# Chunked retention and two feed-forward layers: quarter-array products, and another cut and order of the feed-forward groups

## The chip, the cores and the metric

One core of one Trainium2 chip. The metric is the device time of one execution in microseconds (us), the median of several runs. The kernel before: 912.83 us, the median of 3 runs (910.53 to 913.34).

## The reference

Retention (attention without softmax, with a decay) over 4 batches, 8 heads, 576 tokens, 64 features a head; its output, 2304 tokens by 512 features, goes through two feed-forward layers of 2048 hidden features. Everything is float32.

```
scores = (q @ k.T) / sqrt(64)
ret    = scores * where(i >= j, gamma[h] ** (i - j), 0)
x      = (ret @ v)                        # heads side by side: 2304 x 512
h = x @ w_in;  x = (h * sigmoid(h)) @ w_out
h = x @ w2_in; out = (max(h, 0) + alpha * min(h, 0)) @ w2_out
```

## The kernel before, in words

**Retention.** The 2304 tokens are 18 blocks of 128; a block of 1 MB holds q and k with features on the partitions, and k and v with tokens on the partitions. A block n takes four products, in float32: the scores (`att_scores`, L227: 8 matmuls, 64 rows of the array by 128 columns, 128 tokens streamed), what comes from earlier tokens through a state of 64 x 64 a head ("cross", first loop of `att_out`, L255: 8 matmuls of 64 x 64, 128 tokens streamed), what comes from within the block ("inside", L263: 8 matmuls of 128 x 64, 128 streamed), and the state's update (`att_state`, L268: 8 matmuls of 128 x 64, 64 streamed, accumulated in one PSUM bank over a whole batch). The profile shows a float32 matmul as two passes, each with its weight load. VectorE (DVE) multiplies the scores by a mask, in two halves (L238); GpSimd (POOL) multiplies q by decays (L221) and v by inverse decays (L225); ScalarE (ACT) copies the output (L266) and the state (L277) out of PSUM. The loads go over SyncE's (SP) DMA queue into three buffers.

**Feed-forward.** The tokens are five tiles (256, 512, 512, 512, 512). The 16 hidden feature tiles of a layer are worked in groups of four: for a group and a token tile, four h units (12 matmuls each) and then four y units (`y_unit`, layer 0) or one out unit for each 128 tokens (`out_unit`, layer 1), of 12 matmuls each, which add to what the earlier groups left. Every operand is split into a high and a low float32r part, so that a product takes three matmuls. A token tile is split by `split_x` (L282; ACT copies, DVE subtracts at L288), four times for each group and tile; an h unit ends with a sigmoid on ACT, a product on DVE (L302), a copy on ACT and a difference on DVE (L311).

**Weights.** They come as 64-bit numbers and are converted on the chip: for each weight tile of 128 x 512 two ACT operations, and on DVE a shift (L175), a sign (L180), a mask (L187), a rest (L194) and a low part (L198), with an ACT copy between and a POOL product (L189). These are the jobs of `w_jobs`; `spread` hangs them behind units of the program.

**What sets the order.** The program is a list, `units`, each with the jobs that follow it in `after`; every engine works its own instructions in the order of that list. Blocks stand between units by hand (L407 to L450). The first group needs eight weight tiles; the weights of group g+1 are converted while group g runs over its tiles (L467 to L475).

Of the kernel before, what the change touches and what calls it, by code (L numbers as in the profile page):

```python
# [9 lines left out]
F32 = mybir.dt.float32  # L10
# [8 lines left out]
P = 128  # L19
# [16 lines left out]
def starts_batch(blk):  # L36
    return (blk * P) % S == 0


def boundary(blk):  # L40
    return (blk * P) // S != (blk * P + P - 1) // S


def ends_batch(blk):
    return (blk * P + P) % S == 0
# [14 lines left out]
def retention_ffn_kernel(ctx: ExitStack, tc: tile.TileContext, qkv, w1, w2, alpha, qtab, small, out):  # L60
# [13 lines left out]
    ps = ctx.enter_context(tc.tile_pool(name="ps", bufs=7, space=bass.MemoryType.PSUM))  # L74
    ps_state = ctx.enter_context(tc.tile_pool(name="ps_state", bufs=1, space=bass.MemoryType.PSUM))
# [26 lines left out]
    rings = {k: Ring() for k in ("w0", "w1", "x", "g", "act", "down", "pr")}  # L102
# [4 lines left out]
    rings["act"].grow(big, "act", NMAX, 2)  # L107

# [5 lines left out]
    right = ctx.enter_context(tc.tile_pool(name="right", bufs=1, side="right"))  # L114
    rings["w0"].grow(right, "w0b_", 512, 4, F32R)
    rings["w1"].grow(right, "w1b_", 512, 4, F32R)
    early_pool = ctx.enter_context(ExitStack())
    early = early_pool.enter_context(tc.tile_pool(name="early", bufs=1, side="right"))

    qtab_sb = att.tile([P, NPAIR, S], F32, name="qtab_sb")  # L120
    small_sb = att.tile([P, 2 * P + PERIOD * H], F32, name="small_sb")
    masks = small_sb[:, 0:2 * P].rearrange("p (b t) -> p b t", b=2)
    vtab = small_sb[:, 2 * P:].rearrange("p (n h) -> p n h", h=H)
    state = [att.tile([P, NPAIR, D], F32, name=f"state{i}") for i in range(2)]
    rings["pr"].grow(att, "pr", 4 * P, 4)
    PACK = 4 * DM
    over = NC * NT - 2 * PACK
    packs = [bufb[:, over:over + PACK], bufb[:, over + PACK:], early.tile([P, PACK], F32, name="pack")]

    def pack(n):  # L130
        return packs[n % len(packs)].rearrange("p (s a) -> p s a", s=4)

    def close_att():
        early_pool.close()
        pool = ctx.enter_context(tc.tile_pool(name="weights", bufs=1, side="right"))
        rings["w1"].grow(pool, "w1c_", 512, 4, F32R)
# [8 lines left out]
    def psum(name):  # L145
        return ps.tile([P, 512], F32, tag="ps", name=name)
# [5 lines left out]
    def w_ahead(upto, queue=None):  # L152
        for i in range(len(raws), min(upto, len(worder))):
            layer, kind, f = worder[i]
            raws[i] = stage.tile([P, 512], I64, tag="raw", name="raw", bufs=RAWS)
            (queue or (nc.sync if i < 2 * GF else nc.scalar)).dma_start(out=raws[i], in_=(w1, w2)[layer][kind, f])
# [52 lines left out]
    probs = {}  # L209
    x_hi, x_lo = {}, {}  # L210
    kv = ps_state.tile([P, 512], F32, name="kv")[:, 0:NPAIR * D].rearrange("p (c d) -> p c d", c=NPAIR)
# [3 lines left out]

    def att_prep_q(n, engine):
        q = pack(n)[:, 0].rearrange("p (c t) -> p c t", c=NPAIR)
        at = n * P % S
        for lo, hi in ((0, S - at), (S - at, P)) if at + P > S else ((0, P),):
            a = (at + lo) % S  # L220
            engine.tensor_tensor(out=q[:, :, lo:hi], in0=q[:, :, lo:hi], in1=qtab_sb[:, :, a:a + hi - lo], op=ALU.mult)  # L221

    def att_prep_v(n, engine):
        v = pack(n)[:, 3].rearrange("p (h d) -> p h d", h=H)
        engine.tensor_tensor(out=v, in0=v, in1=vtab[:, n % PERIOD].unsqueeze(2).to_broadcast([P, H, D]), op=ALU.mult)  # L225

    def att_scores(n):  # L227
        q, k = (pack(n)[:, i].rearrange("p (c t) -> p c t", c=NPAIR) for i in range(2))
        sc = [psum("sc").rearrange("p (c t) -> p c t", c=NPAIR) for _ in range(2)]
        for p in range(NPAIR):  # L230
            for j in range(2):
                r = slice(j * D, (j + 1) * D)
                nc.tensor.matmul(sc[j][:, p], k[r, p], q[r, p], start=True, stop=True, skip_group_check=True)  # L233
        mask = masks[:, int(boundary(n))].unsqueeze(1).to_broadcast([P, NPAIR, P])
        probs[n] = []
        for j in range(2):
            pr = rings["pr"].next().rearrange("p (c t) -> p c t", c=NPAIR)
            nc.vector.tensor_tensor(out=pr, in0=sc[j], in1=mask, op=ALU.mult)  # L238
            probs[n].append(pr)

    def att_out(n):
        at = n * P
# [3 lines left out]
        xo = [psum("xo")[:, 0:2 * P].rearrange("p (c t) -> p c t", c=2) for _ in range(2)]  # L246
        begun = set()

        def mm(j, p, cols, lhsT, rhs):
            half = p % 2  # L250
            nc.tensor.matmul(xo[j][half * D:(half + 1) * D, p // 2, 0:cols], lhsT, rhs,  # L251
# [3 lines left out]
        if not starts_batch(n):  # L255
            cols = D if boundary(n) else P
            for p0 in range(0, NPAIR, 2):
                for j in range(2):
                    for p in (p0, p0 + 1):
                        r = slice(j * D, (j + 1) * D)  # L260
# [7 lines left out]
    def att_state(n):  # L268
        if ends_batch(n):
            return  # L270
# [292 lines left out]
```

## Time and profile before

| what | value |
|---|---|
| median of 3 runs | 912.83 us |
| the profiled execution's own time | 912.46 us |
| its span, first to last instruction | 910.7 us |
| mean granted TensorE clock | 0.981 |
| TensorE (PE) busy | 870.2 us (96%) |
| DVE busy | 586.6 us (64%) |
| ACT busy | 434.9 us (48%) |
| POOL busy | 133.7 us (15%) |
| HBM, mean over the span | 64 GB/s |

Busy shares are means over a span of two parts: the stretch in which retention and the first group share the core, up to about 177 us, and the feed-forward after it. The 1.8 us between the profiled time and the span lie outside the instructions.

### The profile page before, as it was taken

How to read it: one execution, taken by the hardware profiler on the slowest of the kernel's cores; microseconds unless marked ns; L12 is line 12 of the kernel's file. 1: busy time of each engine (PE TensorE's matmuls, PEld its weight loads, DVE VectorE, ACT ScalarE, POOL GpSimd, SP SyncE). 2: the span in 40 equal slices, each digit the busy share in tenths (PEclk: the TensorE clock that was granted, in tenths of full speed). 3: DMA queues.
4: the chain of work that ended last, by engine and by line, in shares of the span. 5: the costliest groups of instructions: out<-in, count | busy, mean ns of one | idle time of the engine just before them, and what ended most of it. 6: DMA issues, size and time to landing. Idle time of an engine off the chain costs nothing.

```text
span 910.7 us, 12282 instructions
## 1 busy us (share of the span) xinstructions
PE 870.2 (96%) x4844; PEld 725.4 (80%) x4844; DVE 586.6 (64%) x954; ACT 434.9 (48%) x845; POOL 133.7 (15%) x104
## 2 busy tenths in 40 slices
PE   5749979999999999999999999999999999999998
PEld 4648857788888888888888888888888888888887
DVE  3984354666876677766775666655786677665442
ACT  2534444555543355434544476656555465545340
POOL 2750242210110011110110011010111011100000
PEclk9778989999999999999999999999999999999999
DMA  8630534111211011101101011001201011000102
GB/s 322 223 139 31 177 141 135 60 47 40 70 47 47 1 69 53 41 24 47 62 32 46 1 70 62 32 24 46 70 24 47 24 69 48 24 1 37 55 25 93
DMA packets 18539, 59.31 MB, mean 65 GB/s; under 512 B 2096, under 2 KB 3504, under 8 KB 18480
## 3 DMA queue, kind: packets, MB, share of 16 engines
q10 hardware_dynamic: 8064, 29.36, 9.3%
q1 hardware_dynamic: 10416, 29.15, 9.0%
q8 instruction: 38, 0.62, 0.3%
q14 instruction: 21, 0.17, 0.1%
HBM read 53.78 MB, written 4.72 MB: 64 GB/s over the span
## 4 chain that ended last, share of the span: by engine, by line
PE 90%; DVE 6%; DMA 2%; ACT 1%; issue 1%; SPq 0%; POOL 0%; ACTq 0%; DVEq 0%; POOLq 0%
PE ph L298 14%; PE ph L296 14%; PE ph L297 14%; PE py L321 7%; PE py L322 7%; PE py L323 7%; PE po L342 7%; PE po L341 7%; PE po L340 7%; PE xo L251 2%; PE sc L233 2%; DVE w L198 1%; DMA qtab_sb<-in_qtab 1%; DMA raw<-in_w 1%; DVE a L180 1%; DVE a L194 1%
## 5 line engine op out<-in xcount | busy, mean ns | idle before, releaser
L189 POOL TENSOR_TENSOR low<-low,top 128x512 f32<-128x512 f32 x64 | 89.8, 1404 | 594.2 <-DVE top L187 543.6
L296 PE MATMUL ph<-x,w 128*128 128x512 f32 (+1 forms) x440 | 163.6, 372 | 0.6 <-ACT x L287 0.6
L298 PE MATMUL ph<-x,w 128*128 128x512 f32 (+1 forms) x440 | 163.0, 370 | 1.3 <-DVE x L288 1.3
L297 PE MATMUL ph<-x,w 128*128 128x512 f32 (+1 forms) x440 | 162.7, 370 | 0.0
L298 PEld LDWEIGHTS ph<-x,w 128*128 128x128 f32 x440 | 83.6, 190 | 16.3 <-DVE x L288 2.5
L296 PEld LDWEIGHTS ph<-x,w 128*128 128x128 f32 x440 | 83.8, 190 | 15.3 <-ACT x L287 1.0
L311 DVE TENSOR_TENSOR g<-act,g 128x512 fp32r<-128x512 f32 (+1 forms) x88 | 59.2, 673 | 57.0 <-ACT g L310 57.0
L297 PEld LDWEIGHTS ph<-x,w 128*128 128x128 f32 x440 | 83.8, 190 | 13.9
L307 DVE SCALAR_TENSOR_TENSOR act<-down,nalpha_sb,act 128x512 f32<-128x512 f32 (+1 forms) x80 | 58.9, 737 | 52.6 <-ACT act L306 51.7
L310 ACT CAST g<-act 128x512 fp32r<-128x512 f32 (+1 forms) x88 | 51.2, 582 | 85.2 <-DVE act L302 46.8
L311 DVE TENSOR_TENSOR gb<-act,gb 128x512 fp32r<-128x512 f32 (+1 forms) x72 | 47.2, 655 | 46.0 <-ACT gb L310 46.0
L301 ACT ACTIVATE act<-ph 128x512 f32<-128x512 f32 (+1 forms) x80 | 44.2, 552 | 68.3 <-PE ph L298 68.0
L298 PE MATMUL ph<-x,w0b 128*128 128x512 f32 (+1 forms) x200 | 74.4, 372 | 0.2 <-DVE x L288 0.2
L296 PE MATMUL ph<-x,w0b 128*128 128x512 f32 (+1 forms) x200 | 74.5, 372 | 0.0
L310 ACT CAST gb<-act 128x512 fp32r<-128x512 f32 (+1 forms) x72 | 41.3, 573 | 69.5 <-DVE act L307 39.9
L297 PE MATMUL ph<-x,w0b 128*128 128x512 f32 (+1 forms) x200 | 74.4, 372 | 0.0
L302 DVE TENSOR_TENSOR act<-ph,act 128x512 f32<-128x512 f32 (+1 forms) x80 | 50.8, 634 | 36.3 <-ACT act L301 35.6
L305 ACT ACTIVATE down<-ph 128x512 f32<-128x512 f32 (+1 forms) x80 | 44.1, 551 | 58.8 <-PE ph L298 58.8
L288 DVE TENSOR_TENSOR x<-bufa,x 128x512 fp32r<-128x512 f32 (+1 forms) x80 | 57.3, 721 | 14.6 <-ACT x L287 13.9
L288 DVE TENSOR_TENSOR x<-bufb,x 128x512 fp32r<-128x512 f32 (+1 forms) x80 | 53.1, 664 | 13.7 <-ACT x L287 13.0
L188 ACT CAST w<-a 128x512 fp32r<-128x512 f32 x38 | 23.6, 620 | 70.5 <-DVE a L180 70.5
L321 PE MATMUL py<-g,w 128*128 128x512 f32 (+1 forms) x128 | 48.3, 377 | 7.0 <-ACT g L310 7.0
(129 smaller groups left out, 1860.8 us busy)
## 6 DMA issues: line engine op xcount, KB each, us to landing
raw<-in_w ACTq DMA_DIRECT2D x56, 512.0 KB, 3.2
bufb<-in_qkv SPq DMA_DIRECT2D x24, 512.0 KB, 5.5
pack<-in_qkv SPq DMA_DIRECT2D x12, 512.0 KB, 5.6
out<-bufa SPq DMA_DIRECT2D x17, 256.0 KB, 2.0
raw<-in_w SPq DMA_DIRECT2D x8, 512.0 KB, 4.4
qtab_sb<-in_qtab SPq DMA_DIRECT2D x1, 896.0 KB, 8.4
qtab_sb<-in_qtab SPq DMA_DIRECT2D x1, 256.0 KB, 5.1
out<-bufa SPq DMA_DIRECT2D x2, 128.0 KB, 1.7
```

What stands on the lines that cost most here:

```text
L189: nc.gpsimd.tensor_tensor(out=low, in0=low, in1=top, op=ALU.mult)
L288: nc.vector.tensor_tensor(out=lo, in0=src, in1=f32(hi), op=ALU.subtract)
L296: nc.tensor.matmul(o, wh[:, cs], hi[:, c, 0:n], start=c == 0, stop=False)
L297: nc.tensor.matmul(o, wl[:, cs], hi[:, c, 0:n], start=False, stop=False)
L298: nc.tensor.matmul(o, wh[:, cs], lo[:, c, 0:n], start=False, stop=c == NC - 1)
L310: nc.scalar.copy(gh[:, 0:n], g)
L311: nc.vector.tensor_tensor(out=gl[:, 0:n], in0=g, in1=f32(gh[:, 0:n]), op=ALU.subtract)
L321: nc.tensor.matmul(o, wh[:, ms], gh, start=f == fs[0], stop=False)
L322: nc.tensor.matmul(o, wl[:, ms], gh, start=False, stop=False)
L323: nc.tensor.matmul(o, wh[:, ms], gl, start=False, stop=f == fs[-1])
L340: nc.tensor.matmul(o, gh[:, bs], wh[:, ms], start=f == fs[0], stop=False)
L341: nc.tensor.matmul(o, gh[:, bs], wl[:, ms], start=False, stop=False)
```

## The change

The state is carried from 64 tokens to 64 (`C`, `NCH` = 9 chunks a batch). All four products become 16 matmuls of 64 x 64 that stream 64 columns (8 where a chunk begins or ends a batch), each in one quarter of the array. The decay goes into a table with the mask (`dtab`), applied to the scores in one DVE operation; POOL scales k (`att_prep_k`) instead of v; q is scaled after the scores have read it; its table is built on the chip by one DVE product of 128 x 2048 (`att_tables`). The state's updates are added on DVE, one operation of 128 x 256 for each chunk, and ACT no longer copies the state. A step n (`att_step`) is one unit: cross and half of inside for block n, scores of n+1, the other half of inside, state of n+1, load of block n+4. The blocks have four buffers instead of three. `split_block` splits the 128 tokens of each block behind its step. In PSUM, four single banks serve the units and states, and two pairs the scores and outputs; after retention all eight are single.

Layer 0 has five groups, of 2, 4, 4, 4 and 2 feature tiles, layer 1 four of 4. The order of the tiles turns round at each group of a layer, and the tile at the turn keeps its split x. A unit of a 2-tile group has 6 matmuls in y (h units stay at 12). A step stands behind single units of tiles 0 to 3. A 4-tile group behind a 2-tile group has all eight weight tiles converted ahead of it, else six ahead and two behind.

```diff
-GF = 4
-NG = NF // GF
+C = 64
+NCH = S // C
+GROUPS = [(0, range(0, 2)), (0, range(2, 6)), (0, range(6, 10)), (0, range(10, 14)), (0, range(14, 16)),
+          (1, range(0, 4)), (1, range(4, 8)), (1, range(8, 12)), (1, range(12, 16))]
+PACKS = 4
...
+    def att_scores(n, engine):
+        sc = banks()
         for p in range(NPAIR):
             for j in range(2):
+                for c in range(2):
+                    nc.tensor.matmul(sc[rows(c), j, p * C:(p + 1) * C], k[rows(j), p, rows(c)], q[rows(j), p, rows(c)],
+                                     start=True, stop=True, skip_group_check=True)
+        nc.vector.tensor_tensor(out=probs[n], in0=sc[:, :, 0:NPAIR * C], in1=dtab, op=ALU.mult)
+        att_prep_q(n, engine)
+    def att_state(n):
...
+                for c in cs:
+                    nc.tensor.matmul(up[c][rows(j), p * D:(p + 1) * D], k[rows(c), 2 * p + j], v[rows(c), 2 * p + j],
+                                     start=True, stop=True, skip_group_check=True)
...
+                nc.vector.tensor_tensor(out=new, in0=up[c][:, 0:NPAIR * D], in1=states[g], op=ALU.add)
...
+    def att_step(n):
+        out = att_out(n)
+        next(out)
+        if n + 1 < NBLK:
+            att_prep_k(n + 1, nc.gpsimd)
+            att_scores(n + 1, nc.gpsimd)
+        for _ in out:
+            pass
+        if n + 1 < NBLK:
+            att_state(n + 1)
+        if n + PACKS < NBLK:
+            att_load(n + PACKS)
...
+    for s in range(1, len(TILES)):
+        more = range(n, min(n + 4, NBLK))
+        n += 4
+        first.append(add(hs[s][0]))
+        for i, unit in enumerate(hs[s][1:] + ys[s][0:3]):
+            if i < len(more):
+                at[more[i]] = step(more[i])
+            add(unit)
...
+    spread(w_jobs(0, 2), at[0], first[0])
+    spread(w_jobs(2, 4), first[0], y0)
+    lo, mid = wcut[1]
+    spread(w_jobs(lo, lo + 4), first[1], closed)
+    spread(w_jobs(lo + 4, mid), closed, first[T] + 1)
+    for gi in range(2, len(GROUPS)):
+        lo, mid = wcut[gi]
+        hi = wcut[gi + 1][0]
+        start, end = first[T * (gi - 1)], first[T * gi - 1]
+        spread(w_jobs(lo, mid), first[T * (gi - 1) + 1] + 2, end)
```

On PE, a block's products stand as follows before (block 6 with its neighbours; `sc` scores, `xo` with `state` cross, `xo` with `pr` inside, `kv` the state):

```order
L233 MATMUL sc<-bufb 128x128 x8
L251 MATMUL xo<-bufb,state_123 64x128 x8
L251 MATMUL xo<-pr_125,bufb 64x128 x4
L251 MATMUL xo<-pr_126,bufb 64x128 x4
L275 MATMUL kv<-bufb 64x64 x8
```

And a step now (step 3; the last row stands for the state of a block that ends a batch; in other steps it has 16 matmuls in two banks by turns):

```order
L283 MATMUL two_109<-pack_127,state_120 64x64 x8
L283 MATMUL two_109<-pack_127,state_121 64x64 x8
L283 MATMUL two_109<-pr_119,pack_127 64x64 x8
L245 MATMUL two_108<-bufb 64x64 x16
L283 MATMUL two_109<-pr_119,pack_127 64x64 x8
L259 MATMUL bank_104<-bufb 64x64 x8
```

The forms 128x128 and 64x128 (columns by tokens streamed) are gone; matmuls are 64 now where they were 32.

On DVE, in layer 0, the rows around the second h unit of a tile while the next group's weights are converted, before (L302 and L311 end an h unit, L328 adds a y unit, L288 splits x, the others are weight jobs):

```order
L302 TENSOR_TENSOR act_103<-ph,act_103 128x512
L311 TENSOR_TENSOR g_97<-act_103,g_96 128x512
L288 TENSOR_TENSOR x_93<-bufa,x_92 128x512
L180 SCALAR_TENSOR_TENSOR a<-top,a 128x512
L187 TENSOR_SCALAR top<-a 128x512
L328 TENSOR_TENSOR bufb<-py,bufb 128x512
L288 TENSOR_TENSOR x_93<-bufa,x_92 128x512
L194 TENSOR_TENSOR a<-a,w_2_76 128x512
L328 TENSOR_TENSOR bufb<-py,bufb 128x512
```

And in the last group of layer 0, of two feature tiles, now (L358 and L367 end an h unit, L383 adds a y unit, L335 splits x, L180 to L203 are weight jobs):

```order
L367 TENSOR_TENSOR g_96<-act_99,g_95 128x512
L185 SCALAR_TENSOR_TENSOR a<-top,a 128x512
L192 TENSOR_SCALAR top<-a 128x512
L199 TENSOR_TENSOR a<-a,w0b_1760 128x512
L383 TENSOR_TENSOR bufb<-bank_104,bufb 128x512
L335 TENSOR_TENSOR x_90<-bufa,x_89 128x512
L203 TENSOR_TENSOR w0b_1761<-a,low 128x512
L180 TENSOR_SCALAR a<-top 128x512
L383 TENSOR_TENSOR bufb<-bankb_1774,bufb 128x512
L335 TENSOR_TENSOR x_90<-bufa,x_89 128x512
```

Two or three weight operations stand behind every unit now, where one stood, and a y unit between two L383 rows has 6 matmuls instead of 12.

## Rows read from the trace of the kernel before

**Rows 1.** Busy time by stretch: start:end, length, busy of each engine, clock, DMA.
```profile
core 0: us, PE busy (x) PEld busy (x) DVE busy (x) ACT busy (x) POOL busy (x), PEclk, DMA share, GB/s
23.00:46.00 23.00, 16.44 (x212) 14.68 (x214) 21.34 (x30) 12.02 (x29) 16.42 (x13) 0.78 0.63 219
46.00:69.00 23.00, 11.56 (x94) 9.99 (x93) 19.46 (x28) 7.88 (x20) 11.11 (x8) 0.72 0.37 136
...
300.00:400.00 100.00, 100.00 (x486) 83.94 (x485) 71.30 (x122) 45.47 (x85) 10.96 (x8) 1.00 0.13 43
```

**Rows 2.** Waits of PE: for whom, us in total, times, longest.
```profile
PE sc L233 <- DVE bufb L221: 10.6, 2, 7.2
PE xo L251 <- ACT state L277: 9.1, 4, 3.9
```

**Rows 3.** The chain that ended last, in order of time: start us, us, what.
```profile
68.12 0.58 PE py L322
...
85.98 1.09 PE sc L233 x16
87.07 1.62 PE xo L251 x32
88.69 0.47 PE kv L275 x16
...
176.88 0.43 PE py L321
177.31 0.23 PE py L322
...
907.11 0.12 PE po L340
907.50 0.42 DVE bufa L347
```

**Rows 4.** The timeline of PE: cross products of 128 and of 64 streamed columns.
```profile
87.00 0.67 PE L251 MATMUL xo<-bufb,state 64*64 64x128 f32 x16
...
150.69 0.46 PE L251 MATMUL xo<-bufb,state 64*64 64x64 f32 x16
```

**Rows 5.** DVE by line and shape, 12 to 69 us: busy us, mean ns, idle before.
```profile
L198 DVE TENSOR_TENSOR w<-a,low 128x512 fp32r<-128x512 f32 x8 | 10.1, 1257 | 0.9 <-DVE a L194 0.5
L238 DVE TENSOR_TENSOR pr<-sc,small_sb 128x512 f32<-128x512 f32 x12 | 7.7, 680 | 5.1 <-PE sc L233 5.1
L194 DVE TENSOR_TENSOR a<-a,w 128x512 f32<-128x512 f32 x8 | 7.4, 922 | 0.0
L180 DVE SCALAR_TENSOR_TENSOR a<-top,a 128x512 int32<-128x512 int32 x8 | 7.2, 897 | 0.2
L175 DVE TENSOR_SCALAR a<-top 128x512 int32<-128x512 int32 x8 | 6.1, 762 | 1.2 <-ACT top L167 0.8
L187 DVE TENSOR_SCALAR top<-a 128x512 int32<-128x512 int32 x8 | 3.4, 423 | 0.2
L288 DVE TENSOR_TENSOR x<-bufa,x 128x256 fp32r<-128x256 f32 x4 | 2.1, 544 | 0.0
```

**Rows 6.** POOL by line, 12 to 69 us.
```profile
L189 POOL TENSOR_TENSOR low<-low,top 128x512 f32<-128x512 f32 x8 | 12.2, 1528 | 15.2 <-DVE top L187 15.2
L225 POOL TENSOR_TENSOR bufb<-bufb,small_sb 128x512 f32<-128x512 f32 x5 | 6.3, 1268 | 5.2 <-DMA bufb<-in_qkv 5.2
```

**Rows 7.** DVE by line and shape, 400 to 500 us.
```profile
L288 DVE TENSOR_TENSOR x<-bufa,x 128x512 fp32r<-128x512 f32 x16 | 12.9, 806 | 0.7 <-ACT x L287 0.4
L328 DVE TENSOR_TENSOR bufb<-py,bufb 128x512 f32<-128x512 f32 x16 | 10.9, 685 | 6.2 <-PE py L323 6.2
L311 DVE TENSOR_TENSOR g<-act,g 128x512 fp32r<-128x512 f32 x9 | 6.2, 692 | 6.2 <-ACT g L310 6.2
L180 DVE SCALAR_TENSOR_TENSOR a<-top,a 128x512 int32<-128x512 int32 x8 | 5.5, 685 | 0.1
L187 DVE TENSOR_SCALAR top<-a 128x512 int32<-128x512 int32 x8 | 3.4, 423 | 0.1
```

**Rows 8.** The timeline at the start: start us, us, instruction, idle before.
```profile
8.16 1.04 POOL L225 TENSOR_TENSOR bufb<-bufb,small_sb 128x512 f32<-128x512 f32 x1 [7.72 <-DMA bufb<-in_qkv]
```

More of the change, by code (lines that the diff above doesn't have):

```diff
@@ L268, in att_state @@
-    def att_state(n):
-        if ends_batch(n):
-            return
-        kt, v = (pack(n)[:, i].rearrange("p (h d) -> p h d", h=H) for i in (2, 3))
-        r0 = D if boundary(n) else 0
-        for p in range(NPAIR):
-            for j in range(2):
-                nc.tensor.matmul(kv[j * D:(j + 1) * D, p], kt[r0:, 2 * p + j], v[r0:, 2 * p + j],
-                                 start=p == 0 and (starts_batch(n) or boundary(n)), stop=True, skip_group_check=True)
-        nc.scalar.copy(state[(n + 1) % 2], kv)
+                        mm(j, p, c, v[rows(c), 2 * p + j], pr[rows(c), j, p])
@@ L288, in split_x, with split_block @@
         nc.vector.tensor_tensor(out=lo, in0=src, in1=f32(hi), op=ALU.subtract)
[L290 to L291 removed]
+    def split_block(b):
+        t = next(i for i, (a, m) in enumerate(SPANS) if a <= b * P < a + m)
+        at = b * P - SPANS[t][0]
+        src = acts(bufa, *SPANS[t])[:, :, at:at + P]
+        hi, lo = (t[:, :, at:at + P] for t in x_tiles((0, t)))
+        nc.scalar.copy(hi, src)
+        nc.vector.tensor_tensor(out=lo, in0=src, in1=f32(hi), op=ALU.subtract)
@@ L411, in retention_ffn_kernel @@
-    marks = []
-    for f in range(GF):
-        if f == 0:
-            first.append(len(units))
-        add(hs[0][f])
-        if f < 2:
-            A[4 + f] = block(4 + f)
-    marks.append(len(units))
-    add(*ys[0])
-    first.append(len(units))
-    add(*hs[1])
-    for n in (6, 7):
-        A[n] = block(n)
-    add(*ys[1])
-    A[8] = block(8)
-    for n in (9, 10):
-        A[n] = block(n)
-    first.append(len(units))
-    add(*hs[2])
-    for n in (11, 12):
-        A[n] = block(n)
@@ L432, in retention_ffn_kernel, with step @@
-    add(*ys[2])
-    for n in (13, 14):
-        A[n] = block(n)
-    first.append(len(units))
-    add(*hs[3])
-    for n in (15, 16, 17):
-        A[n] = block(n)
-    closed = len(units)
-    add(close_att)
-    add(*ys[3])
-    first.append(len(units))
-    add(*hs[4])
-    prev = list(ys[4])
+        wcut.append((len(worder), len(worder) + len(a[:early] + b)))
+        worder += a[:2] + b[:2] + a[2:] + b[2:] if gi == 1 else a[:early] + b + a[early:]
+    wcut.append((len(worder),) * 2)
+    def step(n):
+        return add(lambda: att_step(n))
@@ new lines, in retention_ffn_kernel @@
+    hs, ys = zip(*(unit_pair(s) for s in range(len(TILES))))
+    at = {}
+    at[0] = step(0)
+    at[1] = step(1)
+    first.append(add(hs[0][0]))
+    at[2] = step(2)
+    add(hs[0][1])
+    at[3] = step(3)
+    y0 = add(*ys[0][0:2])
+    at[4] = step(4)
+    add(*ys[0][2:4])
+    at[5] = step(5)
+    n = 6
+    for s in range(1, len(TILES)):
[6 more added lines that the diff above has]
+            add(unit)
+        if s < len(TILES) - 1:
+            add(*ys[s][3:])
+        if more and more[-1] == NBLK - 1:
+            closed = add(close_att)
```

309 lines of the change are left out of this document (150 added, 159 removed).

## The prediction, made before the changed kernel had run

> **What bounds the kernel now.** I read the busy time by stretch first [rows 1]. From 300 to 400 us PE is busy for all of it at the full clock, 1.00 (2.4 GHz), and DVE for 71%: from there on only fewer or faster matmuls would help. From 23 to 69 us PE is busy for 28.0 of 46 us at a mean clock of 0.78 and 0.72, so partly at 1.2 GHz, and DVE for 40.8: there DVE sets the pace. The waits of PE [rows 2] are short of that, 10.6 us for q's product on DVE, 9.1 for the copy of the state.
>
> The chain of waits [rows 3] gives two marks. The y units of the first tile run through only from 68.12 us, when DVE has the last of eight weight tiles ready. The last product of retention ends at 176.88. By then tiles 1 and 2 and the h units of tile 3 are done, 240 matmuls of 512 columns, and tile 0, 96 of 256. A matmul of 512 columns takes 0.23 us [rows 3], one of 256 takes 0.12 (the same rows, at the end). So 240 x 0.23 + 96 x 0.12 = 66.7 us of the feed-forward are done at 176.8, and what follows takes 910.7 - 176.8 = 733.9 us to the end of the span. The number of feed-forward matmuls stays the same; I therefore ask when the changed kernel has retention behind it, how much is done by then, and whether PE is kept busy after it.
>
> **Retention on PE.** A block takes 1.09 (scores) + 1.62 (cross and inside) + 0.47 (state) = 3.18 us [rows 3]. The state's 16 passes of 64 columns stand in pairs, one in each half of the array's columns: 0.47 / 8 = 0.058 us a pair. Cross products stand in quarters already. Halving their columns takes them from 0.67 to 0.46 us [rows 4], so that four quarters do overlap, at 64 columns too: 16 passes begin and end in 0.46 us, the fill and end of the pipeline among it. With four at a time, each of the new products (32 passes) takes 8 x 0.058 = 0.46 us, four take 1.86, and with some 0.2 for going in and out between feed-forward units (an estimate, from 3.18 us a block and the 0.1 to 0.2 that the first passes of a form take longer [rows 4]) a step takes 2.05 us. The lower end is 0.67 - 0.46 = 0.21 us for four such rounds [rows 4], 0.053 each, 1.7 a step; the upper end is 32 passes at the state's 0.47 / 16 = 0.029 us, 0.94 a product, 3.75 a step, if no more than two overlap over a long run. I take 2.05, since the nearest row, the same form in quarters, shows four overlapping; the upper end is a rival below.
>
> The Trainium skill says in "TensorE: Matmul & The Clock Gate", section "Wait — 56ns, not 53.3ns?", that matmuls never start closer than about 25 ns however few their columns, and that with decoding in software each costs about 62 ns; by the first a step's 128 passes would take an estimated 3.2 us, by the second 7.9, instead of 2.05. The trace speaks against the second, as a block's 64 passes take 3.18 us, and against the first for a short burst, 16 passes within 0.46 us; for a long run no row here shows it.
>
> **The start, to the first y unit.** The first group needs four weight tiles instead of eight. Until its first y unit DVE has, in its order: four weights at 1.26 + 0.92 + 0.90 + 0.76 + 0.42 = 4.26 us each [rows 5], 17.0; five score products at 0.68 [rows 5], 3.4; nine state updates of 128 x 256, between 0.34 (half of a score product) and 0.68, taken as 0.40, 3.6; four splits of 128 x 512 at 0.85 (0.54 for 128 x 256 [rows 5], and 0.81 for 128 x 512 [rows 7]), 3.4; the ends of two h units, 2.7; the table of 128 x 2048 (four times 0.68 at most, taken as 2.3) with k and q of block 0, 3.3. The sum is 33 us. It begins at about 4 us, when the small table is in. Waits come on top, 8 us: the block's 1.0 MB and the 0.45 of tables ahead of it land at about 8.2 us (before, v of block 0 was the end of 1.45 MB and there at 8.16 [rows 8]), the first products run at half clock, and the weights' loads, now on ACT's queue, stand beside four 1 MB loads. So y begins at **45 us**, where before it ran from 68.
>
> **From there to the end of retention.** Tile 0's four y units (24 matmuls at 0.12, half of them at 1.2 GHz after the wait: 4.3), steps 4 and 5 (4.1, and 1.9 more if one runs at 1.2 GHz) and 2 for block 5's split, which the next h unit awaits at once: tile 1 begins at 57 us. Tiles 1 to 3 take each two h units (24 x 0.227 = 5.45), four y units of 6 matmuls (5.45) and four steps (8.2), 19.1 us. DVE has beside that four times 0.68 + 2 x 0.40 + 0.85 = 9.3, two h units at 0.69 + 0.69 and a wait of 0.69 for ACT between (6.2 us over nine [rows 7]), 4.1, and a third of four weights, at 4.0 each 5.4: 18.8. Both engines are full, and I add 5 us for waits, most for k on POOL, which stands behind a weight's product of 1.53 us [rows 6]. Retention is then done at 57 + 57.4 + 5 = **about 120 us** instead of 177.
>
> **What is done by then** is less, 3 x 48 x 0.227 + 48 x 0.12 = 38.5 us against 66.7: 28.2 more are left, so 733.9 + 28.2 = 762.1 us.
>
> **What two-tile groups cost.** In these groups a token tile is worth 48 x 0.23 = 11.0 us of PE, half of a four-tile group's, but the weights of the next group have to pass DVE in that time. Group 4 (the last of layer 0) has eight of them ahead of layer 1, in 16 units, 2.67 token tiles. DVE has for each token tile: two h ends at 2.07 (4.1), four additions at 0.685 (2.7), four splits at 0.81 (3.2), three weights at 2 x 0.42 + 3 x 0.685 = 2.9 (8.7) [rows 7]: 18.8, and some 17 since neighbours overlap by about 0.08. The order puts the difference that the next y unit reads behind these jobs, with one h unit of 2.76 us between on PE, so PE can't run ahead of DVE by more than about 2 us: (17 - 11) x 2.67 - 2 = **14 us** of stall, where before such a stretch was covered by PE. Behind retention, tile 4 of group 0 has four weights (11.6) and three h ends (6.2) beside 12.4 us of PE: 17.8 - 12.4 - 2 = **3 us**.
>
> The smaller edits: splits saved at the turns cost PE nothing now and give nothing while PE is full (their cover is DVE's slack of 29% there [rows 1]); a fourth block buffer spares waits for loads, which are in the 57 us between the two marks; the end (last addition 0.42 at 907.50 [rows 3], then the store) is the same, half a block.
>
> **Sum.** 120 + 762.1 + 14 + 3 = 899 us of span, and 1.8 outside it: **901 us**. The profiled execution took 912.46, the median of the runs is 912.83, so they stand alike; about 0.3%, 2.7 us, is what a measurement of this kernel can tell from no change.
>
> **The rivals.**
> *Passes come no faster than 0.029 us.* Quarters overlap in a burst, but not over 64 matmuls in a row. For it: the longest run of quarters in the trace has 16 passes, after a pause. Against it: nothing slows in that run. Its place is the 14 steps from the first y on. Each takes 3.75 + 0.2 = 3.95 instead of 2.05, 26 us in all; the 5 us of waits vanish beneath it: 901 + 26 - 5 = 922 us, slower than before. It decides from about 2.9 us a step on.
> *The copies out of PSUM and the decays hold up retention.* The order of a step puts the state's addition and q's scaling between the scores and the next cross product; where before PE waited 9.1 us in four waits for a state [rows 2], it waits now in each of 12 steps, 1 us more than I count: 913 us, no change. For it: DVE at 18.8 of 19.1. The Trainium skill's "TensorEngine Tiling (Array Packing)", section "PSUM Bottleneck", warns of this: packing speeds up TensorE, not the way out of PSUM.
> *The weights' jobs find room.* If DVE's work in the two-tile groups is covered (its queue runs ahead or ends overlap more), 14 of the 17 us go: 887 us.
> *The steps don't pack at all* would give the price of the first rival; the change's other parts stand in the order either way.
>
> **How the numbers follow.** Forecast 901 us, with 893 to 910 of its own: 50%. Passes too slow, 922: 17%. Retention held up, 913: 15%. Weights covered, 887: 18%. Faster by over 0.3% (below 910): 0.45 from the first, 0.18 from the last, 0.63. Within 0.3%: 0.05 and 0.08, 0.13. Slower: 0.17 and 0.07, 0.24. The range leaves out some 10% on either side: below, the half of the covered case that gains further in retention, above, the worse half of slow passes: 885 to 921.
>
> **What would show it.** In the new profile: a product's 32 passes in about 0.46 us, a step in about 2; the first y unit at about 45 us; retention done at about 120; gaps of PE in the last group of layer 0, some 14 us together, laid to the difference on DVE; none after it. Passes of 0.029 us, or retention past 135 us, or a full PE in that group would make the forecast wrong.

## The result, and the profile after

| what | before | after |
|---|---|---|
| median of the runs | 912.6 us (910.53 to 913.34, 4 runs) | 924.46 us (923.61 to 925.07, 4 runs) |
| ratio to before, 95% interval | | 1.0133 [1.0114, 1.0152] |
| span of the profiled execution | 910.7 us | 923.3 us |
| mean granted TensorE clock | 0.981 | 0.972 |
| PE busy | 870.2 us (96%) | 868.2 us (94%) |
| DVE busy | 586.6 us (64%) | 594.4 us (64%) |
| ACT busy | 434.9 us (48%) | 428.8 us (46%) |
| POOL busy | 133.7 us (15%) | 128.7 us (14%) |

The changed kernel is 1.3% slower than before, where 901 us, 1.3% faster, was forecast; the time lies above the range (885 to 921). I read the new profile at the marks of the forecast first, then by stretch, then by waits.

The marks, from the timeline of PE (start us, us, instruction, idle before and what ended it): the first y unit runs through from 44.47, tile 1 begins at 54.19, the last product of retention starts at 132.11, and 135.35 is the first h unit after tile 3.

```profile
44.47 0.58 PE L377 MATMUL bank<-g,w 128*128 128x256 f32 x1 [0.39 <-DVE w L203]
...
54.19 0.50 PE L352 MATMUL bank<-x,w 128*128 128x512 f32 x1 [0.68 <-ACT x L343]
...
132.11 0.46 PE L283 MATMUL two<-pr,pack 64*64 64x64 f32 x16 [0.50 <-ACT bufa L303]
...
135.35 0.39 PE L352 MATMUL bankb<-x,w 128*128 128x512 f32 x1
```

Forecast were 45, 57 and 120 for the first, second and last of these. So the start came as worked out, and the stretch from tile 1 to the end of tile 3 took 81.2 us instead of 62.4 (57.4 and 5 of waits).

PE by stretch (start:end, length, busy time, clock, DMA):

```profile
core 0: us, PE busy (x), PEclk, DMA share, GB/s
0.00:54.00 54.00, 30.30 (x832) 0.81 0.63 234
54.00:136.00 82.00, 67.39 (x1539) 0.94 0.42 143
136.00:460.00 324.00, 322.14 (x1550) 0.99 0.12 40
460.00:512.00 52.00, 41.72 (x140) 0.84 0.22 78
512.00:923.00 411.00, 406.68 (x1874) 1.00 0.12 42
```

Two stretches lose time: the one with retention, and the last group of layer 0 at 460 to 512 us. In the latter 140 matmuls, all of 512 columns, at the 0.23 us of a covered one [rows 3] are 32.2 us of 52: 19.8 us are lost, of which 10.3 with PE idle and the rest in slower matmuls at a mean clock of 0.84. The long stretches beside it are full: 1.9 us idle in 324, 4.3 in 411.

All engines in the stretch with retention:

```profile
core 0: us, PE busy (x) PEld busy (x) DVE busy (x) ACT busy (x) POOL busy (x), PEclk, DMA share, GB/s
54.00:136.00 82.00, 67.39 (x1539) 53.38 (x1540) 48.18 (x76) 36.81 (x74) 30.70 (x27) 0.94 0.42 143
```

No engine is full here. DVE is busy for 48.2 us of 82, where I had it at 18.8 of each 19.1 us, 56.4 of 57.4 (4.1 of these were waits for ACT within the h units). The time goes into waits of PE, which that stretch lists so (for whom, us in total, times, longest):

```profile
PE two L283 <- ACT bufa L303: 8.2, 8, 2.1
PE bank L259 <- POOL pack L230: 4.9, 3, 1.9
...
PE two L283 <- DVE state L267: 0.5, 1, 0.5
```

With the two rows left out, 0.7 us each, that is 15.0 us instead of 5. Over the whole span the same view has:

```profile
PE two L283 <- ACT bufa L303: 14.1, 11, 3.1
...
PE bank L259 <- POOL pack L230: 5.4, 4, 1.9
...
PE bank L259 <- POOL bufb L230: 1.8, 1, 1.8
```

These take the place of the waits of [rows 2], which are gone. The largest, for ACT's copy at L303, is not a wait for a state or for DVE. The timeline of all engines around one step that stands behind an h unit shows it (rows of the weight loads are left out):

```profile
92.78 0.69 PE L283 MATMUL two<-pack,state 64*64 64x64 f32 x32
92.89 0.60 ACT L357 ACTIVATE act<-bank 128x512 f32<-128x512 f32 x1 [1.26 <-PE bank L354]
...
93.30 0.41 PE L283 MATMUL two<-pr,pack 64*64 64x64 f32 x16
...
93.52 0.69 DVE L358 TENSOR_TENSOR act<-bank,act 128x512 f32<-128x512 f32 x1
93.53 0.65 PE L245 MATMUL two<-bufb 64*64 64x64 f32 x32
94.24 0.62 ACT L366 CAST g<-act 128x512 fp32r<-128x512 f32 x1 [0.76 <-DVE act L358]
...
94.77 0.37 ACT L303 COPY bufa<-two 128x256 f32<-128x256 f32 x1
...
95.19 0.46 PE L283 MATMUL two<-pr,pack 64*64 64x64 f32 x16 [1.01 <-ACT bufa L303]
...
95.47 0.65 PE L259 MATMUL bank<-bufb 64*64 64x64 f32 x32
...
96.04 0.50 PE L376 MATMUL bank<-g,w 128*128 128x512 f32 x1
```

A step puts out the cross products and the first half of the inside products (16 matmuls), the scores of the next block, and then the second half of inside. That half adds to the same banks from the other half of the array's rows, and the program lets ACT copy the first sums out before it. The copy stands in ACT's queue behind the end of the h unit: the sigmoid (92.89), DVE's product with it (93.52), and the cast that waits for this product (94.24). So PE waits from 94.18 to 95.19 for a copy of 0.37 us. The state's product behind it waits in other steps for k, which POOL scales.

The arithmetic itself packs. The 32 matmuls of the scores at 93.53 take 0.65 us to the end of the last; one alone is shown as 0.22 us long (the row at 87.52 us in experiment 5), so they start within 0.43 us, 14 ns apart. The ends of matmuls are modelled in a profile; the starts alone say nearly the same, 48 passes between 92.78 and 93.53, 16 ns apart. From 92.78 to 96.04 are 3.26 us, without the wait 2.25; 2.05 was forecast.

**Where the time went between the two kernels.** At the end of retention before had 66.7 us of the feed-forward done of 176.8, and now 38.5 of 135.35. So retention with all that surrounds it costs 96.9 us instead of 110.1, 13.2 less. The rest takes 923.3 - 135.35 = 787.95, less the 28.2 that it has more to do 759.8, against 733.9: 25.9 more. The difference is the 12.6 us of the two spans. The change gains in retention, though little, and gives twice as much back behind it, 19.8 us of that in one group.

### The profile page after: what moved, and what is told of

Same layout as the page of the kernel before. It is cut to its first block, busy times and chain, and to the rows that moved or that the text cites. A ratio compares the mean times of both kernels' runs of the same rounds, so it can differ in the third digit from the quotient of the medians.

```text
span 923.3 us, 14365 instructions
## 1 busy us (share of the span) xinstructions
PE 868.2 (94%) x5932; PEld 714.8 (77%) x5932; DVE 594.4 (64%) x979; ACT 428.8 (46%) x819; POOL 128.7 (14%) x102
## 4 chain that ended last, share of the span: by engine, by line
PE 84%; DVE 10%; ACT 3%; issue 1%; POOL 1%; DMA 1%; ACTq 0%; SPq 0%; DVEq 0%; POOLq 0%
PE bankb L353 9%; PE bankb L354 9%; PE bankb L352 9%; PE bank L376 7%; PE bank L377 6%; PE bank L378 6%; PE bank L354 5%; PE bank L353 5%; PE bank L352 5%; PE bankb L396 4%; PE bankb L394 4%; PE bankb L395 4%; PE bank L396 3%; PE bank L395 3%; PE bank L394 3%
## 5 line engine op out<-in xcount | busy, mean ns | idle before, releaser
L194 POOL TENSOR_TENSOR low<-low,top 128x512 f32<-128x512 f32 x64 | 89.2, 1393 | 630.5 <-DVE top L192 593.7
L354 PE MATMUL bankb<-x,w 128*128 128x512 f32 (+1 forms) x276 | 103.2, 374 | 1.9 <-DVE x L335 1.9
L353 PE MATMUL bankb<-x,w 128*128 128x512 f32 (+1 forms) x276 | 102.9, 373 | 1.5 <-DVE w L203 1.5
L352 PE MATMUL bankb<-x,w 128*128 128x512 f32 (+1 forms) x276 | 102.9, 373 | 0.0
L363 DVE SCALAR_TENSOR_TENSOR act<-down,nalpha_sb,act 128x512 f32<-128x512 f32 (+1 forms) x80 | 61.8, 772 | 51.3 <-ACT act L362 50.3
L367 DVE TENSOR_TENSOR g<-act,g 128x512 fp32r<-128x512 f32 (+1 forms) x84 | 57.4, 683 | 54.2 <-ACT g L366 54.2
L366 ACT CAST g<-act 128x512 fp32r<-128x512 f32 (+1 forms) x84 | 48.7, 579 | 78.4 <-DVE act L358 39.8
L367 DVE TENSOR_TENSOR gb<-act,gb 128x512 fp32r<-128x512 f32 (+1 forms) x76 | 48.7, 641 | 48.8 <-ACT gb L366 48.8
L357 ACT ACTIVATE act<-bankb 128x512 f32<-128x512 f32 (+1 forms) x65 | 35.9, 552 | 69.8 <-PE bankb L354 69.7
L383 DVE TENSOR_TENSOR bufb<-bank,bufb 128x512 f32<-128x512 f32 (+1 forms) x69 | 44.2, 641 | 35.4 <-PE bank L378 35.1
L353 PE MATMUL bank<-x,w 128*128 128x512 f32 (+1 forms) x164 | 60.5, 369 | 4.5 <-DVE w L203 4.5
L354 PE MATMUL bank<-x,w 128*128 128x512 f32 (+1 forms) x164 | 61.1, 373 | 3.3 <-DVE x L335 2.6
L352 PE MATMUL bank<-x,w 128*128 128x512 f32 (+1 forms) x164 | 61.3, 374 | 1.6 <-ACT x L334 0.9
L354 PEld LDWEIGHTS bankb<-x,w 128*128 128x128 f32 x276 | 51.9, 188 | 12.3 <-DVE x L335 3.2
L353 PEld LDWEIGHTS bankb<-x,w 128*128 128x128 f32 x276 | 51.9, 188 | 10.9 <-DVE w L203 1.7
L358 DVE TENSOR_TENSOR act<-bankb,act 128x512 f32<-128x512 f32 (+1 forms) x65 | 41.3, 635 | 29.0 <-ACT act L357 28.2
L352 PEld LDWEIGHTS bankb<-x,w 128*128 128x128 f32 x276 | 51.9, 188 | 9.3
L335 DVE TENSOR_TENSOR x<-bufb,x 128x512 fp32r<-128x512 f32 (+1 forms) x68 | 46.8, 689 | 9.7 <-ACT x L334 9.1
L353 PE MATMUL bankb<-x,w0b 128*128 128x512 f32 (+1 forms) x136 | 50.0, 368 | 0.0
L352 PE MATMUL bankb<-x,w0b 128*128 128x512 f32 (+1 forms) x136 | 50.0, 368 | 0.0
```

Source lines behind the costliest of these rows:

```text
L194: nc.gpsimd.tensor_tensor(out=low, in0=low, in1=top, op=ALU.mult)
L352: nc.tensor.matmul(o, wh[:, cs], hi[:, c, 0:n], start=c == 0, stop=False)
L353: nc.tensor.matmul(o, wl[:, cs], hi[:, c, 0:n], start=False, stop=False)
L354: nc.tensor.matmul(o, wh[:, cs], lo[:, c, 0:n], start=False, stop=c == NC - 1)
L363: nc.vector.scalar_tensor_tensor(out=g, in0=dn, scalar=nalpha_sb[:, f:f + 1], in1=g, op0=ALU.mult, op1=ALU.add)
L366: nc.scalar.copy(gh[:, 0:n], g)
```

## The experiments

Ratios are against before, run beside each experiment on the same chip (911.95 to 912.6 us on all of them). "After" stands for the changed kernel, 924.46 us and 1.0133.

**1. Groups of three in place of the last two-tile group.**

```diff
-GROUPS = [(0, range(0, 2)), (0, range(2, 6)), (0, range(6, 10)), (0, range(10, 14)), (0, range(14, 16)),
+GROUPS = [(0, range(0, 2)), (0, range(2, 6)), (0, range(6, 10)), (0, range(10, 13)), (0, range(13, 16)),
```

> One edit: layer 0 in groups of 2, 4, 4, 3 and 3 feature tiles instead of 2, 4, 4, 4 and 2. Ahead of layer 1 stand seven weight tiles in three quarters of a group's time, not eight in half of it. Theory A: the gaps and the half clock in the last group of layer 0 (about 14 us of gaps and 6 of clock between 463 and 510 us) come from DVE's eight weights there: they go but for 2 or 3, 906 us. Rival B: they come from something else at the change of layers (splits of x, the order of the tiles): still some 20 us there, 924 us.

Measured: 912.78 us (910.81 to 915.39, 10 runs), 1.0001 [0.9988, 1.0013], 11.7 us below after. The same place in its profile, by stretch:

```profile
core 0: us, PE busy (x), PEclk, DMA share, GB/s
457.00:512.00 55.00, 52.36 (x238) 0.97 0.12 39
```

Of these 238 matmuls 190 have 512 columns and 48 have 256. At 0.23 and 0.12 us they are 49.5 us of work in 55, so 5.5 us are lost here instead of 19.8, at a clock of 0.97. Counted by the same matmuls, from the first of the fourth group to the third h unit of layer 1, the profile has 173.1 us instead of 184.0 in after. Seven weight tiles pass DVE in the last group, instead of eight, in a group that is half as long again. More than half of the loss in that group is so shown to come from its size (the one weight fewer follows from it), and 11.7 us are nearly the whole of the difference to before.

**2. The state's products ahead of the second half of inside.**

```diff
-        for _ in out:
-            pass
         if n + 1 < NBLK:
             att_state(n + 1)
+        for _ in out:
+            pass
```

> One edit: in a step the state's products of block n+1 stand ahead of the second half of inside, not behind it. Theory A: a step loses time because the second half of inside waits for ACT's copy of the first half (14.1 us in 11 waits of the changed kernel), and that wait is counted from the end of the first half; 0.45 us more of PE work between them takes 0.45 us from each long wait and all of the short ones of 0.2: 11 x 0.45, about 5 to 6 us less, 918 to 920 us. Rival B: in retention DVE and ACT are full whatever PE does, the time returns at the next cross product or state: 924 us, unchanged. If the state then waits for k on POOL, up to 0.3 us a step come back.

Measured: 924.67 us (921.79 to 931.11, 4 runs), 1.0145 [1.0099, 1.0191]: no gain that runs so far apart can show. Its waits of PE over the span:

```profile
PE bank L259 <- POOL pack L230: 9.8, 4, 2.6
...
PE two L283 <- ACT bufa L303: 5.9, 7, 1.7
PE bank L259 <- POOL bufb L230: 5.3, 1, 5.3
```

The wait for the copy fell from 14.1 to 5.9 us, and that for k rose from 7.2 to 15.1. The two waits lay one behind the other; what stands first takes the time of both.

**3. k a step earlier on POOL.**

```diff
-            att_prep_k(n + 1, nc.gpsimd)
             att_scores(n + 1, nc.gpsimd)
+        if n + 2 < NBLK:
+            att_prep_k(n + 2, nc.gpsimd)
```

> One edit: POOL scales k of block n+2 behind q of block n+1, a step earlier, so that it no longer queues behind a weight's product that waits for DVE. Theory A: the 7.2 us that the state's products wait for POOL in the changed kernel go, but a part is only the lead of another wait in the same step: 917 to 921 us. Rival B: POOL has no time left, q comes later instead: 924 us or above.

Measured: 918.54 us (918.21 to 921.1, 4 runs), 1.0074 [1.0054, 1.0094], 5.9 us below after. No wait for POOL at L230 is left in its profile, and the other stands where it stood:

```profile
PE two L283 <- ACT bufa L303: 14.1, 11, 3.6
```

The gain is near the 7.2 us that the view gave for this wait. Not all of it is PE's idle time: between the starts of tiles 1 and 4 that falls from 14.4 to 13.1 us only, and the clock there is 1.00 instead of 0.94 (the table further down).

**4. The h unit's end queued behind the next step's first copy.** In retention the sigmoid and what follows it are put off until the step has issued its first copy:

```diff
         out = att_out(n)
         next(out)
+        while pending:
+            pending.pop(0)()
...
+        if defers[0] and (layer, f) in ((0, 0), (0, 1)):
+            pending.append(lambda: h_end(key, layer, f, n, o))
+        else:
+            h_end(key, layer, f, n, o)
```

> One edit: in retention an h unit's end (sigmoid, product, copy, difference) is issued behind the next step's first copy out of PSUM instead of ahead of it, so that this copy doesn't queue on ACT behind a copy that waits for DVE's product. Theory A: the long waits of 1.23 us that stand in the steps behind h units fall to the 0.24 of the steps behind y units; six of them in tiles 1 to 3 and two in tile 0, 8 x 1.0 = 8 us less, but the y unit behind the second h unit gets its operand 0.8 us later, 3 x 0.8 = 2 us back: 918 us. Rival B: DVE is what limits, the h unit's end comes later and everything behind it too: 924 us or above.

Measured: 921.19 us (919.2 to 923.95, 4 runs), 1.0101 [1.0071, 1.013]: 3.3 us below after, and the intervals overlap. Its waits (its lines L285, L261 and L387 are L283, L259 and L376 of after):

```profile
PE bank L387 <- ACT g L377: 5.9, 4, 1.9
PE bank L261 <- POOL pack L232: 5.8, 4, 2.2
PE two L285 <- ACT bufa L305: 5.5, 4, 3.1
```

The wait for the copy went from 14.1 us in 11 to 5.5 in 4. That the copy was late for its place in ACT's queue is so shown. But the y unit behind the step now waits for g, 5.9 us instead of the 3.0 that L376 had in after, since the h unit's end now begins later. Between the starts of tiles 1 and 4 PE's idle time falls from 14.4 to 10.8 us.

**5. Two quarters at a time.** The loops are turned so that neighbouring matmuls alternate between two quarters in the scores and the state; the other loops are turned too, but their neighbours overlapped as before.

```diff
-        for p in range(NPAIR):
-            for j in range(2):
-                for c in range(2):
+        for c in range(2):
+            for p in range(NPAIR):
+                for j in range(2):
```

> One edit to the changed kernel: the same matmuls in another order, so that each of the four products uses two quarters of the array at a time and then the other two. Theory A (quarters overlap four at a time, as the step's rows of 0.43 us a product say): a product takes 0.9 us instead of 0.45, a step 1.8 us more; what of it lies in the wait for ACT's copy (the scores' 0.45) costs nothing, so about 1.2 us over 16 steps, some 20 us: 944 us. Rival: PE is not what limits retention, the waits shrink by what the products grow: 924 to 930 us.

Measured: 927.29 us (925.41 to 928.74, 4 runs), 1.0174 [1.0157, 1.0191], 2.8 us above after. Its timeline of PE in one step:

```profile
87.52 0.22 PE L245 MATMUL two<-pack 64*64 64x64 f32 x1
...
87.58 0.92 PE L245 MATMUL two<-pack 64*64 64x64 f32 x31
89.17 0.48 PE L283 MATMUL two<-pr,pack 64*64 64x64 f32 x16 [0.68 <-ACT bufa L303]
89.45 0.93 PE L259 MATMUL bank<-pack 64*64 64x64 f32 x32
```

The scores take 0.98 us and the state 0.93, where each took 0.65 in after. That is 0.6 us in a step, some 8 us over 14 steps, and the kernel loses a third of it: the scores' part lies within the time of the wait for the copy behind them, which falls from 8.2 us to 5.9 in the stretch from 54 to 136 us. So the pace that the first rival feared, in two of the four products, cost 2.8 us, where its price for all four was 26; all four at that pace were not run.

**6. Without the turn of the tiles.** `order = range(len(TILES))` in every group.

> One edit: the tiles run in the order 0 to 4 in every group, as in the kernel before, so that no tile at a turn keeps its split x. Theory A: at the turns DVE has slack but behind retention and in the last group of layer 0; there four more splits of 0.7 us and the short first tile cost 2 to 6 us: 926 to 930 us. Rival B: the turn itself costs (the weights of the next group must be ready sooner behind the last tile): 924 us or below.

Measured: 925.95 us (924.64 to 928.28, 4 runs), 1.0157 [1.0138, 1.0176]. The interval overlaps that of after, and by the medians the turn is worth 1.5 us. The two profiles differ ahead of tile 4, where the program is the same, by 2.8 us the other way; from there to the end of the span this run takes 790.8 us and after 787.95, so the turn gives some 2.9 us, as theory A had it.

**7. A first group of four.** Layer 0 in four groups of four, with k a step earlier; the start's list has all four h units, with a step behind each, ahead of the y units. The edit also puts all eight weights of the next group behind retention, where before and after have four of them beside it.

```diff
-GROUPS = [(0, range(0, 2)), (0, range(2, 6)), (0, range(6, 10)), (0, range(10, 14)), (0, range(14, 16)),
+GROUPS = [(0, range(0, 4)), (0, range(4, 8)), (0, range(8, 12)), (0, range(12, 16)),
...
-    spread(w_jobs(lo, lo + 4), first[1], closed)
-    spread(w_jobs(lo + 4, mid), closed, first[T] + 1)
+    spread(w_jobs(lo, mid), closed, first[T] - 1)
+    spread(w_jobs(mid, lo + 8), first[T] - 1, first[T] + 3)
```

> Layer 0 in four groups of four, as in the kernel before, with the new retention and k a step earlier: the first group needs eight weight tiles again, but each step stands beside twice the feed-forward work. Theory A (retention is held up by a fixed way from an h unit through ACT and DVE to the copies, a price for each step): more feed-forward between the steps hides nothing of it, the first y unit comes some 15 us later, and no group of two tiles is left to overload DVE: the start loses what the groups give, 915 us or above. Rival B: the waits of the steps are short of work for PE; with two more h units for each tile they are filled: 906 us or below.

Measured: 930.68 us (929.61 to 931.26, 4 runs), 1.0207 [1.019, 1.0224]. The y units run through from 68.3 us, as before (68.12 [rows 3]), and the waits of PE grow:

```profile
PE two L283 <- ACT bufa L303: 30.7, 17, 4.8
PE bank L377 <- ACT g L367: 8.2, 3, 4.2
```

The kernel is 18.7 us slower than before, and 23.1 us above experiment 9, which has the other cut. The wait for the copy more than doubles: in tiles 1 to 3 all four steps stand behind h units here. Retention is done sooner than before all the same: the y unit behind its last product starts at 170.08 us, with the same feed-forward work done that before had at 176.88. The kernel loses its time behind that, in the tiles after retention:

```profile
core 0: us, PE busy (x), PEclk, DMA share, GB/s
190.00:240.00 50.00, 36.10 (x129) 0.83 0.19 64
```

These 129 matmuls of 512 columns are 29.7 us of work at 0.23; 20.3 are lost, with waits for g and for a weight among the jobs that the edit put there. So this run does not measure the first group's size alone. Of the 23.1 us some 14 arise up to the end of retention (170.08 - 66.7 = 103.4 us besides the feed-forward work, 127.66 - 38.5 = 89.2 in experiment 9) and 9 behind it, where the weights stand elsewhere too.

**8. The edits together.** Groups of three, the state's products moved (2) and k earlier (3):

> Three edits together: groups of 2, 4, 4, 3, 3, the state's products ahead of the second half of inside, and k scaled a step earlier. Theory A: the first alone took 11.7 us, the third 5.9; the second gave 8 us at ACT's copy and lost 8 at POOL's k, which the third takes away: 924.5 - 11.7 - 5.9 - 6 = 901 us. Rival B: with those waits gone DVE is what limits retention: 906 us, what the first and third give.

Measured: 906.45 us (903.54 to 909.28, 5 runs), 0.9934 [0.991, 0.9959]: faster than both kernels. The first h unit behind tile 3 starts at 127.67 us, not 120. Waits of PE that are left in the steps:

```profile
PE two L283 <- ACT bufa L303: 11.3, 11, 3.1
...
PE two L283 <- DVE state L267: 2.6, 4, 1.0
```

With the put-off h end (4) added:

> As the run with three edits, and an h unit's end is issued behind the next step's first copy. Theory A: the copy comes 1 us sooner behind h units, of which the moved state has taken 0.45 already; the y unit waits longer for its operand. Alone it gave 3.3 us, most of it in the same wait: 1 to 2 us less than the run with three edits, 899 us. Rival B: its new wait at the y unit is as long as what it saves: no less than the run with three edits.

Measured: 908.44 us (904.45 to 909.15, 6 runs), 0.9952 [0.9935, 0.9968], no better. PE waits less between 54 and 136 us, but the clock there is 0.90, where the run with three edits has 0.98 and after 0.94:

```profile
54.00:136.00 82.00, 74.05 (x1561) 0.90 0.42 148
```

**9. Without the moved state.** Groups of three and k earlier alone:

> Two edits: groups of 2, 4, 4, 3, 3 and k a step earlier, the state's products left behind the second half of inside. Theory A: the moved state is worth nothing, since the wait for ACT's copy only changes its place (to the next cross product, through the second copy): 924.5 - 11.7 - 5.9 = 907 us, the same as with the moved state (906.5). Rival B: the moved state is worth 3 to 6 us once POOL no longer holds it up: 910 us or above.

Measured: 907.56 us (905.73 to 910.6, 10 runs), 0.9955 [0.994, 0.9969]. The two edits add up: 924.46 - 11.7 - 5.9 = 906.9. The moved state is worth nothing that these runs can tell.

**10. Other places for the steps.** Experiment 9 with each step of a tile one unit later, behind the second h unit and the first three y units:

> As the run with two edits, and the four steps of a tile stand behind its second h unit and its first three y units, not behind both h units and two y units. Theory A (the long wait for the first copy, 1.2 us, belongs to steps behind h units, 0.2 to those behind y units): one long wait less for each of three tiles, 3 us less, and 1 to 2 us more where the next tile's first h unit waits for the last block's split, which one y unit alone now covers: 905 us. Rival B: the waits don't depend on the unit ahead: 907 us or above.

Measured: 909.95 us (905.84 to 912.64, 10 runs), 0.9976 [0.996, 0.9992], 2.4 us above experiment 9 with intervals that overlap: no gain.

**11. Weight jobs later.** Experiment 8, with two of the weights spread a tile later behind retention, and two of the seven ahead of layer 1 moved into its first tile:

> The run with three edits, and two more in the place of weight jobs: behind retention the last two weights of group 1 follow a tile later, and two of the seven weights ahead of layer 1 follow at its first tile. Theory A (in the small groups PE waits because the jobs stand ahead of the differences that the next y unit reads): the gaps at 133 to 137 us (2.4 us) and in the last group of layer 0 (4.6 us) go but for 1 or 2: 901 us. Rival B: the same DVE work only stalls later, at the next y units: 906 us.

Measured: 907.09 us (904.74 to 909.94, 6 runs), 0.9942 [0.9923, 0.9961], the same as experiment 8. But its two moves pull against each other. From the second h unit of the last group of layer 0 to the third of layer 1, 375 matmuls take 76.95 us, full and at a clock of 1.00, where experiment 8 has 82.97 with PE busy for 79.74 at 0.98: two weights fewer to convert there give 6.0 us back, as theory A had it (1.4 are lost again in layer 1). Behind retention, tile 4 and group 1 take 5.0 us more than in experiment 8. The second move alone was not run. The gap behind retention, which I had laid to DVE's jobs, stayed. The chain of waits there (start us, us, what):

```profile
136.84 0.62 ACT w0b L193
137.45 0.51 ACT act L358
...
137.98 0.70 DVE act L359
...
138.71 0.63 ACT g L367
...
139.38 0.79 PE bankb L377
```

Behind a weight's cast stands the plain way from the h unit to its y unit: sigmoid, product, cast. With two h units in a group and no step between, PE has nothing to cover the second one's way.

## Why the prediction was wrong, by its own steps

**Passes, 0.46 us a product: right.** 0.65 us to the end of the last pass, 0.43 from first start to last. The trace so settles what no row of before could: the floor of about 25 ns between matmuls in the Trainium skill's "TensorE: Matmul & The Clock Gate", section "Wait — 56ns, not 53.3ns?", would make an estimated 0.80 us of 32 passes, and the measured 0.43 lies under it. Neighbours here stand in different quarters. The prediction's row for a short burst, 16 passes within 0.46 us, did not yet speak against that floor, by which 16 passes start within an estimated 0.40.

**The start, 45 us: right,** at 44.5, and tile 1 at 54.2 instead of 57. In part this is luck: up to 44.47 us DVE was busy for 28.3 us instead of 33, and from its first operation at 4.11 it waited for 12.1 instead of 8. The copy at L303 already held PE up for 5.8 us in three waits, which the forecast did not have.

**"Tiles 1 to 3 ... 19.1 us ... Both engines are full, and I add 5 us for waits": this step failed.** It took 81.2 us instead of 62.4. I compared the work of PE with that of DVE and took the larger, and left out the chain within a step: first half of inside, copy on ACT, second half, with this copy behind the end of an h unit in ACT's queue. DVE was not full, busy for 47.7 of the 81.2 us. Of the 18.8 us too much, 9.4 are idle time of PE, 14.4 us instead of 5; of its waits 8.2 us are laid to the copy, for which the sum has no term. Another 4.0 are the clock: experiment 3 has the same matmuls of this stretch in 62.7 us of busy time at 1.00, after in 66.7 at 0.94, and the forecast had no such term behind the start. The other 5.4 are matmul time above the 57.3 forecast. Passes that run out ahead of a wait make some 2.4 of that (12 steps of 2.25 instead of 2.05); 3.0 are not assigned.

The same stretch, from the first h unit of tile 1 to that of tile 4, in the other profiles:

| run | length, us | PE idle, us | clock |
|---|---|---|---|
| after | 81.2 | 14.4 | 0.94 |
| experiments 1 and 6 (same program here) | 79.5, 78.3 | 14.5, 14.5 | 0.96, 0.98 |
| 2, state moved | 77.6 | 14.4 | 0.98 |
| 3, k earlier | 75.8 | 13.1 | 1.00 |
| 4, h unit's end put off | 78.2 | 10.8 | 0.96 |
| 8, with three edits | 73.8 | 10.2 | 0.98 |
| 8, with four edits | 77.0 | 8.3 | 0.89 |

One program takes 78.3 to 81.2 us here, by its clock; its idle time is the same to 0.1 us. So the idle time tells more of an edit than the length. Experiment 4 takes away 7.3 of the 8.2 us of waits for the copy and 3.6 us of idle time; experiment 2 moves the wait and takes nothing. That the step's chain through ACT and POOL holds PE up is so shown, but not that it makes the whole excess: no run comes below 73.8 us, where 62.4 was forecast.

**The wait for k, "most" of the 5 us: right in kind,** 4.9 us in the stretch, and experiment 3 gets back 5.9 overall.

**Two-tile groups, 14 + 3 us: right in mechanism and place, too small in size.** 19.8 us in the last group of layer 0: DVE is busy for 46.2 of the 52, and the timeline of all engines there shows PE waiting for the difference and for g, as forecast. Behind some of these waits it also shows runs of slower matmuls, which were not forecast.

```profile
483.24 0.68 DVE L335 TENSOR_TENSOR x<-bufa,x 128x512 fp32r<-128x512 f32 x1
...
483.98 0.79 PE L354 MATMUL bank<-x,w 128*128 128x512 f32 x1 [1.37 <-DVE x L335]
...
484.57 0.63 PE L376 MATMUL bank<-g,w1b 128*128 128x512 f32 x1
...
484.99 0.63 PE L377 MATMUL bank<-g,w1b 128*128 128x512 f32 x1
...
487.10 0.80 PE L376 MATMUL bank<-g,w1b 128*128 128x512 f32 x1 [1.05 <-ACT g L366]
```

These matmuls start some 0.43 us apart instead of 0.23, and from 484 to 492.5 us the granted clock is 0.50, the 1.2 GHz level; it is 0.53 from 469 to 472.6 and from 506.5 to 510. Not every wait is followed by this: behind one of 1.36 us at 502.35 the matmuls start 0.23 apart. Experiment 1 gets 11.7 us of the term back, and experiment 11 shows the weights' jobs to be the cause: with two of them taken out, PE has no idle time left in the last group of three feature tiles, from its second h unit on. In tile 4 of group 0 PE has 1.9 us idle between 136 and 460 us, with a clock of 0.99 (at most 3.2 us more), about the 3 forecast. In experiment 11's chain this gap is the h unit's own way behind a weight's cast; how much of it is DVE's load, as forecast, is not shown.

**The sum.** 15.4 us too late at the end of retention and 8.8 too much after it (787.95 instead of 779.1) make the 24 us between 899 and 923.

**The rivals.** Slow passes fell by the timeline, and by experiment 5 their price looks too high as well. Covered weights fell by the 19.8 us of the last group and by experiment 1. The second, copies and decays that hold up retention, came nearest: 10 us of waits more than counted, where it said 12. Its heading names copies out of PSUM, but it priced the state's addition and q's scaling, and PE's waits for those are 0.5 us in the stretch; the copy of the inside products and k's scaling took their place. The Trainium skill's "TensorEngine Tiling (Array Packing)", section "PSUM Bottleneck", which says that packing speeds up TensorE and not the way out of PSUM, is borne out: by experiment 5 half the packing of scores and state is worth 2.8 us. It failed to hold the time because it stood alone: the forecast let either retention or the groups go wrong, and both did.

**What stays open.** Experiment 8 has retention behind it at 127.7 us and not at 120, with 11.3 us of waits for the copy over its span. Edits that shorten this wait moved a part of it or all of it (experiments 2, 4, 8). Whether both halves of inside can follow each other without ACT's copy between them was not tried. Nor was the smaller first group alone, with the weights of the next group left where they are.

## What to carry to other kernels

Before an engine's sums decide what bounds a stretch, follow one iteration's chain through the queues of all engines: PE waited 8.2 us for a 0.37 us copy that stands behind a sigmoid's end, though no engine was more than 82% busy, and putting the copy first took 3.6 us off PE's idle time. When a group of work is made smaller to start earlier, count what has to pass the other engines during it everywhere it is used: here 13.2 us were gained up to the end of retention and 25.9 lost behind it, and another size of the last group alone gave 11.7 back. And if two waits stand one behind the other, take away the one whose producer can run a step earlier (k on POOL); moving the consumers only changed the wait's name here.

## What the runs showed of the hardware that was not expected

Matmuls of 64 x 64 in the four quarters start 14 ns apart over 32 in a row; with two quarters by turns 32 take 0.93 us to the end of the last, 23 ns apart.

A DVE product between two SBUF tiles, L367, took 0.69 us at 487.08 and 1.28 at 94.89, where POOL worked on SBUF from 94.36 to 95.63 and from 95.58 on, as these two rows of the step above show:

```profile
94.36 1.27 POOL L236 TENSOR_TENSOR bufb<-bufb,qtab 128x512 f32<-128x512 f32 x1 [3.53 <-PE two L245]
...
94.89 1.28 DVE L367 TENSOR_TENSOR g<-act,g 128x512 fp32r<-128x512 f32 x1 [0.68 <-ACT g L366]
```

A product that reads PSUM, L358, stayed at 0.69 us at 485.70 beside a POOL product that ran from 485.15 to 486.71. The rest of after's trace agrees: of the L367 rows that write g at this size, 62 with next to no POOL work beside them took 0.69 or 0.70 us and five with POOL work for more than half of their time 1.28, while L383, which reads PSUM, took 0.68 or 0.69 in either case (46 and 10 rows). No experiment was made on this.
